# Transposes moved from TensorE to VectorE as 32x32 blocks, and a projection on eight small TensorE tiles

## The chip, the cores and the metric

The kernel runs on one core of one Trainium2 chip. The metric is the device time of one execution in microseconds (us); lower is better. In the profile, PE is TensorE's matmuls, PEld its weight loads, DVE is VectorE, ACT is ScalarE, POOL is GpSimd and SP is SyncE; L472 is line 472 of the kernel that the profile belongs to.

## The reference, cut to what matters

```python
# x: [8, 4224, 192] f32; weight: [8, 7]; w_q, w_k: [192, 64]; w_out: [192, 192]
w   = softmax(weight, axis=-1)                        # 7 taps for each of 8 heads of 24 features
y   = causal convolution of x along the 4224 tokens, with the taps of each feature's head
wq, wk = y @ w_q, y @ w_k
mixed  = (1/sqrt(64)) * (wq @ wk.T) @ y               # no softmax, so the order may be changed
out    = relu(mixed) @ w_out                          # [8, 4224, 192] f32
```

There is no softmax in the mixer. So the kernel forms the small matrix `G = y.T @ y` and from it `M = scale * w_k.T @ G`, and gets `mixed = (y @ w_q) @ M`. Its stages per batch are Y (convolution as a banded matmul), G, M, Q (`y @ w_q`, kept transposed), Z (`relu`), and O (`@ w_out`, then the store).

## The kernel before

The 4224 tokens of a batch are two halves of 2112, worked on side by side. Each half is cut into 18 chunks of 122 tokens. Y leaves tokens on partitions, and Q needs features on partitions, so there is a transpose stage T between them. T runs on TensorE, as matmuls with an identity:

```python
def job_t(b, k):                       # two chunks; 9 such jobs per batch
    def pe(e, bk):
        bank = PS[:, bk, :].bitcast(BF16)
        for q in range(2):
            ...
            for s_ in range(3):        # 3 x 128 of the 384 features (both halves of the tokens)
                last = e.transpose(bank[:, o0 : o0 + m],
                                   Y[0:m, b % 2, c, first : first + 128], IDENT[0:m, 0:m])
        return last
    # evicted: 3 x 244 bf16 columns PSUM -> YT

def job_q(b, k):                       # 488 columns; 5 such jobs per batch
    ...
        for s_, wt in enumerate((WQA, WQB, WQT)):          # full 128x128 weights
            last = e.matmul(PS[:, bk, o0 : o0 + w], wt, y[:, s_], start=..., stop=s_ == 2, ...)
    # evicted: PSUM -> QT
```

A stored tile holds 512 tokens of both halves, four tokens to a partition, and goes out in one DMA:

```python
            elif q == 1:
                src = OUT[:, orr, :, :]                     # 128 partitions x 2 halves x 3072 bytes
                dst = bass.AP(out_t, (b * S + 512 * i) * D,
                              [[4 * D, 128], [HALF * D, 2], [1, 4 * D]])
            ...
            st = P.dma("sp", lambda e: e.dma_start(dst, src), og[orr], evs)
```

All engines run fixed lists of instructions. When the program is built, a scheduler puts one job after another, by a priority for each stage (`KEYS`) and by estimated costs. It gives each eviction from PSUM to the one of VectorE and ScalarE that would finish it first:

```python
COST = {"act": (0.1, 0.833e-3, 0.833e-3), "dve": (0.1, 1.04e-3, 0.52e-3)}   # us, us per element
...
eng = min(("act", "dve"), key=lambda e_: end[e_])
```

## Time and profile before

| | before |
|---|---|
| time, median of the first three runs | 195.45 us (194.65 to 198.22; the run of 198.22 counts as slow) |
| span of the profiled run | 194.0 us, mean granted TensorE clock 0.990 |
| first Y matmul; last eviction; end | 11.76; 188.99; 194.0 us |
| one batch in steady state | 21.8 us |

These are lines from the page of the profile before. The first four are the span in 40 slices, with each digit the busy share of a slice in tenths (PEclk: granted clock). The last two are the chain of work that ended last, by engine and by line, as shares of the span.

```profile
PE   7749999999999999999999999999999999999980
DVE  4864586737856497737966496737856496736740
ACT  2354288876987597876877588876987588875990
PEclk9988999999999999999999999999999999999999
...
PE 89%; DVE 4%; POOL 2%; ACT 1%; issue 1%; POOLq 0%
PE ps L472 13%; PE ps L599 12%; PE ps L442 12%; PE ps L397 11%; PE ps L601 11%; PE ps L493 7%; PE ps L562 6%; PE ps L494 6%; PE ps L495 4%; PE ps L577 4%; DVE shift L296 1%; ACT y L729 1%; POOL xw L205 1%; PE ps L526 1%; DVE xw L369 0%
```

PE is full from slice 4 to slice 38, and the chain stays on it for 89% of the span. The chain in order of time (start, duration, what) shows a repeating mark, a pair of transpose groups:

```profile
55.79 0.65 PE ps L442 x12
...
77.54 0.65 PE ps L442 x12
...
99.28 0.65 PE ps L442 x12
```

So a batch takes 21.8 us. The view by stretches, asked for two of these periods, gives the length and then the busy time of each engine with its number of instructions:

```profile
55.79:77.54 21.75, 21.63 (x227) 16.72 (x225) 14.96 (x29) 16.80 (x34) 4.72 (x6) 1.00 1.37 264
77.54:99.28 21.74, 21.62 (x225) 16.71 (x225) 14.97 (x29) 16.79 (x34) 0.00 (x0) 1.00 1.37 264
```

The columns are PE, PEld, DVE, ACT, POOL, clock, DMA share and GB/s. VectorE and ScalarE have 5 to 7 us to spare in each period. The groups of instructions, with shapes kept apart, show what T and Q cost and what VectorE needs per element (count, then busy us and mean ns of one, then idle time before them and its releasers):

```profile
L734 DVE TENSOR_SCALAR zt<-ps 128x512 bf16<-128x512 f32 x68 | 45.5, 686 | 15.1 <-PE ps L577 5.4 <-PE ps L601 5.1 <-PE ps L562 4.5
L729 DVE COPY yt<-ps 128x732 bf16<-128x732 bf16 x64 | 34.3, 536 | 17.4 <-PE ps L442 9.8 <-PE ps L577 6.8
L442 PE MATMUL ps<-ident,y 122*128 122x122 bf16 x408 | 33.5, 216 | 0.0
L472 PE MATMUL ps<-yt,wall 128*128 128x244 bf16 x192 | 25.6, 268 | 0.3
...
L734 DVE TENSOR_SCALAR zt<-ps 128x64 bf16<-128x64 f32 x9 | 1.9, 222 | 4.1 <-PE ps L562 4.0
```

The mean ns of a matmul is its latency and not its cost, since the next one starts long before it ends. For the cost one reads distances between starts. In the trace they are 54 ns for 122 columns, 83 for 192, 106 for 244, 163 for 384, 183 for 432 and about 216 for 512 (medians). Summed over a batch, everything but T and Q needs about 15.6 us of PE, T needs 2.9 and Q 2.8. That is 21.3 of the 21.8 us.

One more reading matters below. The prediction used the closest starts in the trace, those of the 64-column matmuls in the timeline:

```profile
69.50 0.19 PE L528 MATMUL ps<-gs,wall 128*128 128x64 bf16 x1
69.53 0.19 PE L529 MATMUL ps<-gs,wall 128*128 128x64 bf16 x1
69.56 0.19 PE L530 MATMUL ps<-gs,wall 128*128 128x64 bf16 x1
```

### The profile page before, as it was taken

To read this page: it belongs to the slowest core of one execution; us is meant where nothing else is said; L and a number is where in the kernel's file an instruction comes from. 1 tells how busy PE (TensorE), PEld (TensorE's weight loads), DVE (VectorE), ACT (ScalarE), POOL (GpSimd) and SP (SyncE) were. 2 spreads that over 40 slices of the span, in tenths; PEclk is the share of its full clock that TensorE was granted. 3 is DMA by queue.
4 is the path that set the end of the run, shared out by engine and by line. 5 is a ranking of instruction groups with operands and counts; after the bars stand their busy time and mean duration, and the time that the engine had idled before them with its cause. 6 is when DMAs were issued, how large, how long until landed. Compare 5 with 4: busy or idle time off the path is not lost.

```text
span 194.0 us, 4387 instructions
## 1 busy us (share of the span) xinstructions
PE 181.9 (94%) x1799; PEld 138.3 (71%) x1814; DVE 125.5 (65%) x254; ACT 139.3 (72%) x273; POOL 46.2 (24%) x74
## 2 busy tenths in 40 slices
PE   7749999999999999999999999999999999999980
PEld 2218957788588957788578966788588967789650
DVE  4864586737856497737966496737856496736740
ACT  2354288876987597876877588876987588875990
POOL 6649999992532200000000000000000000000000
PEclk9988999999999999999999999999999999999999
DMA  2996999999999999999999993346044623346098
GB/s 35 182 200 58 192 187 191 272 273 283 269 224 252 276 333 198 271 270 290 263 217 266 286 300 131 124 176 250 0 166 162 268 80 138 114 180 243 0 381 288
DMA packets 47683, 40.21 MB, mean 207 GB/s; under 512 B 37936, under 2 KB 39728, under 8 KB 47664
## 3 DMA queue, kind: packets, MB, share of 16 engines
q0 software_dynamic: 36480, 13.63, 59.1%
q1 hardware_dynamic: 11184, 26.31, 37.3%
q8 instruction: 14, 0.23, 0.4%
q14 instruction: 5, 0.04, 0.1%
HBM read 27.60 MB, written 25.95 MB: 276 GB/s over the span
## 4 chain that ended last, share of the span: by engine, by line
PE 89%; DVE 4%; POOL 2%; ACT 1%; issue 1%; POOLq 0%
PE ps L472 13%; PE ps L599 12%; PE ps L442 12%; PE ps L397 11%; PE ps L601 11%; PE ps L493 7%; PE ps L562 6%; PE ps L494 6%; PE ps L495 4%; PE ps L577 4%; DVE shift L296 1%; ACT y L729 1%; POOL xw L205 1%; PE ps L526 1%; DVE xw L369 0%
## 5 line engine op out<-in xcount | busy, mean ns | idle before, releaser
L729 ACT COPY o_sb<-ps 128x768 f32<-128x768 f32 (+1 forms) x69 | 52.7, 767 | 17.8 <-PE ps L601 15.2
L734 DVE TENSOR_SCALAR zt<-ps 128x512 bf16<-128x512 f32 (+1 forms) x77 | 47.4, 632 | 19.2 <-PE ps L562 8.4
L729 ACT CAST y<-ps 128x432 bf16<-128x432 f32 (+2 forms) x110 | 46.1, 477 | 10.1 <-PE ps L397 9.7
L729 DVE COPY yt<-ps 128x732 bf16<-128x732 bf16 (+1 forms) x65 | 34.6, 534 | 17.4 <-PE ps L442 9.8
L599 PE MATMUL ps<-wall,zt 128*128 128x192 bf16 x272 | 44.9, 247 | 0.0
L601 PE MATMUL ps<-wall,zt 128*128 128x384 bf16 x136 | 44.3, 326 | 0.0
L397 PE MATMUL ps<-xw,band 128*128 128x432 bf16 x128 | 36.7, 351 | 3.3 <-DVE zt L371 3.3
L493 PE MATMUL ps<-y 128*128 128x192 bf16 x144 | 34.8, 249 | 1.1 <-ACT y L729 0.7
L599 PEld LDWEIGHTS ps<-wall,zt 128*128 128x128 bf16 x272 | 27.7, 113 | 10.2 <-ACT o_sb L729 2.0
L494 PE MATMUL ps<-y 128*128 128x192 bf16 x144 | 34.7, 248 | 0.0
L442 PE MATMUL ps<-ident,y 122*128 122x122 bf16 (+1 forms) x432 | 33.7, 216 | 0.0
L205 POOL DMA_DIRECT2D xw<-in_x_dram x32 | 30.2, 1008 | 12.5 <-issue 12.5
L495 PE MATMUL ps<-y 128*128 128x128 bf16 x144 | 31.8, 221 | 0.0
L442 PEld LDWEIGHTS ps<-ident,y 122*128 122x128 bf16 (+1 forms) x432 | 27.5, 97 | 3.5
L472 PE MATMUL ps<-yt,wall 128*128 128x244 bf16 (+1 forms) x216 | 28.5, 265 | 0.3
L729 DVE CAST y<-ps 128x432 bf16<-128x432 f32 x34 | 20.4, 604 | 8.9 <-PE ps L397 8.8
L472 PEld LDWEIGHTS ps<-yt,wall 128*128 128x128 bf16 x216 | 18.2, 97 | 7.5 <-DVE yt L729 4.2
L562 PE MATMUL ps<-qt,m_sb 128*128 128x512 bf16 (+1 forms) x65 | 21.1, 333 | 0.5
L729 ACT CAST qt<-ps 128x488 bf16<-128x488 f32 x25 | 14.1, 565 | 8.7 <-PE ps L472 8.6
L732 ACT ACTIVATE zt<-ps 128x512 bf16<-128x512 f32 (+1 forms) x43 | 19.1, 479 | 1.5 <-PE ps L562 1.5
L493 PEld LDWEIGHTS ps<-y 128*128 128x128 bf16 x144 | 14.2, 99 | 4.8 <-DVE y L729 1.4
L494 PEld LDWEIGHTS ps<-y 128*128 128x128 bf16 x144 | 14.2, 99 | 3.6
(65 smaller groups left out, 150.8 us busy)
## 6 DMA issues: line engine op xcount, KB each, us to landing
out_dram<-o_sb SPq DMA_DIRECT2D x31, 768.0 KB, 6.9
xw<-in_x_dram POOLq DMA_DIRECT2D x24, 384.0 KB, 26.0
xw<-in_x_dram POOLq DMA_DIRECT2D x8, 432.0 KB, 26.2
out_dram<-o_sb SPq DMA_DIRECT2D x8, 96.0 KB, 5.0
out_dram<-o_sb SPq DMA_DIRECT2D x2, 384.0 KB, 4.0
xw<-in_x_dram POOLq DMA_DIRECT2D x8, 45.8 KB, 19.6
xw<-in_x_dram POOLq DMA_DIRECT2D x16, 16.5 KB, 28.8
wst<-in_moe_w_out_dram SPq DMA_DIRECT2D x1, 96.0 KB, 6.1
```

What stands on the lines that cost most here:

```text
L205: return e.dma_start(XW[:, b % NX, slot : slot + n, :], bass.AP(x_t, base, [[D, 128], [CW * D, n], [1, D]]),)
L397: return e.matmul(PS[:, k, 0:432], BAND[:, h, :], rhs, start=True, stop=True)
L442: last = e.transpose(bank[:, o0 : o0 + m], Y[0:m, b % 2, c, first : first + 128], IDENT[0:m, 0:m],)
L472: last = e.matmul(PS[:, bk, o0 : o0 + w], wt, y[:, s_], start=s_ == 0 and j == 0, stop=s_ == 2, skip_group_check=True)
L493: e.matmul(PS[:, 7, 0:192], y[:, 0:128], y[:, 0:192], start=c == 0, **fl)
L494: e.matmul(PS[:, 7, 192:384], y[:, 256:384], y[:, 192:384], start=False, **fl)
L495: return e.matmul(PS[:, 7, 384:512], y[:, 128:256], y[:, 128:256], start=False, **fl)
L562: return e.matmul(PS[:, bk, 0:w], M_SB[:, b % 2, 256 * h : 256 * h + 128], QT[:, b % 2, s0 : s0 + w], start=True, stop=True)
L599: e.matmul(o[:, 192 * h : 192 * h + 192], ZT[:, zr, h, cols], WO1, start=h == 0, stop=False, **kw)
L601: last = e.matmul(o[:, 0:384], ZT[:, zr, 2, cols], WO2, start=False, stop=True, **kw)
L729: last = e.copy(o, i) if eng == "act" else e.tensor_copy(o, i)
L734: last = e.tensor_scalar(o, i, 0.0, None, op0=ALU.max)
```

## The change

The intent is to take the transposes off the engine that bounds the kernel. VectorE can transpose 32x32 blocks inside SBUF. Features then lie on groups of 32 partitions, each group with other tokens. So Q no longer has a contraction over 128 rows. It becomes six accumulating matmuls of 32 rows by 64 columns for each of four row groups (tokens) and two column halves (the two halves of the sequence), which is eight tiles of the array. Chunks shrink from 122 to 120 tokens, so that a chunk is a whole number of four-token groups. The order of the tokens in `QT` changes with that, and so each store now goes out by chunks. Evictions of Y are merged in pairs (864 columns), and a Q job takes four PSUM banks at once.

```diff
-    CW = 122
+    CW = 120
-        rows = 6 + LAST if c0 == NCK - 1 else 128
+        rows = 6 + (LAST if c0 == NCK - 1 else CW)         # loads of 126 partitions
...
+    def job_td(b, k):                                      # three chunks; 6 such jobs per batch
+        def make(bk):
+            return [(
+                YB[:, g, c : c + 3, :].rearrange("p c d -> p (c d)"),
+                Y[:, b % 2, 3 * k : 3 * k + 3, :].rearrange("p c d -> p (c d)"),
+            )]
+        ...  evacs=[(make, ("TD", b, k), 1152, False, "transpose")]      # e.transpose on VectorE
...
+    def job_q(b, g):                                       # 2 such jobs per batch
         def pe(e, bk):
+            for j in range(6):
+                for i in range(4):
+                    r = slice(32 * i, 32 * i + 32)
+                    for h in range(2):
+                        blk = j if h == 0 else (8 + j if j < 4 else 2 + j)
+                        rhs = YB[r, g, :, 32 * blk : 32 * blk + 32]
+                        last = e.matmul(PS[64 * h : 64 * h + 64, bk + i, 0:288], WQ[r, j, :], rhs,
+                                        start=j == 0, stop=j == 5, skip_group_check=True)
...
+            for h in range(2):                             # stores: 14 DMAs per batch, not 5
+                if rem:
+                    parts = [(0, 64, row(h, 17 * CW), [[D, 64], [1, D]])]
+                elif i < 3:
+                    parts = [(0, 128, row(h, 32 * i), [[CW * D, 16]] + chunk)]
+                else:
+                    parts = [
+                        (0, 96, row(h, 96), [[CW * D, 16], [4 * D, 6], [1, 4 * D]]),
+                        (96, 126, row(h, 16 * CW), [[4 * D, 30], [1, 4 * D]]),
+                        (126, 128, row(h, 17 * CW + 64), [[4 * D, 2], [1, 4 * D]]),
+                    ]
```

The priorities of the stages were set anew with it (Y starts earlier, O later: 1.24 instead of 1.05), and the scheduler counts a Q job as 1.6 us.

## The prediction

> **What bounds the kernel now.** TensorE. The chain of waits gives PE 89% of the span. In the stretches by time, every 22 us stretch from 30 to 184 us has PE busy 21.8 to 21.9 us, VectorE about 14.7 and ScalarE 17.3 (together 32.2 of 44). The chain repeats the double transpose group at 55.79, 77.54, 99.28, 121.16, 142.93 and 164.74 us: one batch costs 21.8 us of PE time. Eight of them are 174 us; about 12 us of start and 8 us of drain make up the rest. DMA holds nobody up in steady state.
>
> **Removed from PE, per batch.** By the timeline's starts, a group of six transposes takes 0.32 us, nine groups 2.9 us; Q takes 0.63 us per 488 columns, 2.7 us. Without both, PE needs 16.2 us.
>
> **Added to PE.** Per batch two Q jobs of 48 weight loads and 48 matmuls of 288 columns, eight tiles at once. With perfect overlap a job would be six rounds of about 0.12 us. The densest load-and-matmul pairs in the trace (the 64-column ones of the small product) start 0.03 us apart; 48 pairs at that rate are 1.45 us. The Trainium skill, "TensorEngine Tiling (Array Packing)", Key Properties, says that tiles load weights and multiply in parallel and that a change of tiling mode drains the array; no run here shows either yet. My estimate: 1.65 us a job plus some 0.15 us of drain, 3.6 us per batch. PE then needs about 19.8 us.
>
> **Moved to VectorE and ScalarE, per batch.** The evictions of the transposes go: (34.6 + 3.9)/8 = 4.8 us. Six VectorE transposes of 128x1152 come. The Trainium skill, "Vector Engine (DVE) Microarchitecture Reference", section 3.8, gives one element per cycle and lane. The trace's evictions of 512 and 64 columns (686 and 222 ns) give 1.04 ns per element and 0.16 us fixed, so about 1.35 us each, 8.1 us. Merged Y evictions (864 wide) save six fixed costs, 1.0 us; Q's eviction falls into eleven pieces instead of five and gives that back. Sum 32.2 - 4.8 + 8.1 = 35.5 us, 17.7 us per engine: 90% of a 19.8 us period. That leaves little slack, and Q needs four PSUM banks at once. I add 0.2 us of PE stalls: period about 20.0 us (removed 5.6, added 3.6 and 0.2).
>
> **Lost.** Stores grow from 41 to about 112 issues of about 0.4 us, harmless in steady state, but after the last evictions eight issues instead of two lengthen the tail: about +2 us.
>
> **Sum.** 195.5 - 8 x 1.8 + 2 = about 183 us. Range (8 in 10): 173 to 192 us. Chances: faster by over 2% 0.80, within 2% 0.13, slower 0.07.
>
> **What will show it.** PE still near the limit, period 19 to 20.5 us; a Q job spans 1.4 to 1.9 us from its first to its last start; VectorE transposes 48 x about 1.3 us (some 63 us busy, VectorE total up by some 25 us); last eviction to end about 7 us instead of 5.
>
> **What would make it wrong.** Weight loads of the small tiles in series (over 2.5 us a job) would eat the gain: 193 to 198 us. A Q job under 1 us would hand the bound to VectorE and ScalarE, near 172 us. A VectorE transpose much slower than an element per cycle, or PE waiting for the transposes and four free banks, would move the period to VectorE, above 190 us.

## The result

| | before | after |
|---|---|---|
| time, median | 195.28 us (4 runs, one of them slow) | 186.89 us (4 runs, one of them slow; a fifth is slow too) |
| ratio | | 0.957, 95% interval 0.951 to 0.963 |
| span of the profile; mean clock | 194.0 us; 0.990 | 185.6 us; 0.961 |
| first Y matmul | 11.76 us | 13.70 us |
| last eviction | 188.99 us | 174.70 us |
| last eviction to end | 5.1 us | 10.9 us |
| one batch in steady state | 21.8 us | 19.3 us |

A ratio is the mean time of one kernel's runs over that of the other's runs of the same rounds, so it is not quite the ratio of the medians quoted beside it. Executions over 1.5% slower than the fastest of the same kernel are left out of the means.

The kernel became faster by 4.3%. The table says where: the stretch from the first Y matmul to the last eviction shrank by 16.2 us (177.2 to 161.0), the start grew by 1.9 us and the tail by 5.8 us. The net is 8.4 us.

The same lines of the page, after:

```profile
PE   7907977998998999979989999799899999799500
DVE  4846786998699779985998689968995899767100
ACT  2114739985998789868997899769986998599600
PEclk9995799999999999999999999999999999999965
...
PE 42%; DVE 25%; ACT 18%; DMA 6%; issue 2%; POOL 1%; ACTq 0%
DVE yb L780 19%; PE ps L623 9%; PE ps L403 7%; PE ps L625 7%; PE ps L466 6%; DMA xw<-in_x_dram 6%; ACT o_sb L782 6%; ACT zt L785 5%; ACT y L782 5%; PE ps L586 3%; DVE zt L787 3%; PE ps L517 2%; PE ps L518 2%; PE ps L601 2%; ACT qt L782 2%
```

The chain no longer stays on PE. It goes through three engines, and VectorE's transposes (L780) are the largest single part. The clock falls in slices 4 and 5, after PE stood idle through slice 3, and the last two slices have no compute at all. The fall is deeper than before the change. These are the same 9 us of the start, before and then after (the columns are explained above):

```profile
12.00:21.00 9.00, 8.30 (x76) 6.19 (x75) 5.26 (x10) 5.39 (x13) 8.49 (x16) 0.81 1.06 118
12.00:21.00 9.00, 6.15 (x24) 3.03 (x25) 5.45 (x5) 3.48 (x7) 6.92 (x13) 0.62 0.89 101
```

The mean granted clock was 0.81 and 0.62 there. An estimate from that: 9 us at these clocks are worth 1.7 us less than at full clock before the change, and 3.4 us less after it. The loss varies between profiles. In the traces of the 14 profiles, the first stretch at half clock took 3.4, 6.8 or 10.2 us; it took 10.2 us in the five in which PE stood idle longest before the first Y matmul (5.2 to 5.7 us; 3.3 to 4.6 us in the others). Two profiles, gap_08 and q_one_tile, have a second stretch after 26 us. So single profiles may differ by 1.7 or 3.4 us from this alone. The periods below lie where the clock is 1.00 and are free of it.

Two stretches of two batches each, from one first Q job to that of two batches later:

```profile
82.02:120.61 38.59, 36.70 (x479) 25.41 (x479) 33.04 (x54) 33.39 (x64) 0.00 (x0) 1.00 1.31 268
120.61:159.20 38.59, 36.70 (x480) 25.42 (x479) 33.03 (x54) 33.39 (x64) 0.00 (x0) 1.00 0.58 172
```

A batch takes 19.3 us. PE is busy in 95% of that, VectorE in 86% and ScalarE in 87%. Busy PE counts latencies. By the distances between starts, PE needs 15.6 us for what did not change and, as the next views show, 2 x 0.87 us for Q: 17.35 us. So PE loses some 1.9 us per batch, where before it lost 0.5. The groups of the new work:

```profile
L780 DVE STREAM_TRANSPOSE yb<-y 128x1152 bf16<-128x1152 bf16 x48 | 62.6, 1349 | 0.4
...
L466 PE MATMUL ps<-yb,wq 32*64 32x288 bf16 x768 | 15.1, 285 | 1.2 <-DVE zt L787 0.6 <-DVE yb L780 0.5
```

The timeline of PE around the first Q job (start, duration):

```profile
22.90 0.94 PE L466 MATMUL ps<-yb,wq 32*64 32x288 bf16 x48
23.77 0.26 PE L517 MATMUL ps<-y 128*128 128x192 bf16 x1
```

The next matmul starts 0.87 us after the job's first. In the single records eight matmuls start 3 to 4 ns apart, the next eight follow 123 ns after the first eight (147 ns in most later jobs), and so on for six rounds (0.66 us from the first start to the last). About 0.21 us passes from the last start to the next ordinary matmul, of which 0.12 us are its own 288 columns.

The chain within a period shows the new handover between the engines:

```profile
102.03 0.87 PE ps L466 x48
...
110.18 0.67 DVE zt L787
110.85 3.81 DVE yb L780 x3
114.69 0.32 DVE y L812
115.04 0.69 DVE zt L787
115.76 3.90 DVE yb L780 x3
119.66 0.59 DVE zt L787
120.29 0.39 PE ps L601
120.68 0.87 PE ps L466 x48
```

VectorE transposes for 3.8 to 3.9 us on end, three blocks in a row, and evicts nothing meanwhile. At 119.66 it empties the bank that a Z matmul (L601) waits for, and the next Q job comes after that. The timeline shows PE's wait of 1.04 us:

```profile
120.29 0.39 PE L601 MATMUL ps<-qt,m_sb 128*128 128x512 bf16 x1 [1.04 <-DVE zt L787]
120.61 0.94 PE L466 MATMUL ps<-yb,wq 32*64 32x288 bf16 x48
```

It shows one thing more. The Q job starts 0.32 us after a matmul of 512 columns, where the next ordinary one starts after about 0.216. In all twelve jobs before which PE did not wait, the first start comes 0.09 to 0.12 us later than usual. So a Q job costs PE about 0.1 us on entering as well, and 0.2 of the 1.9 us per batch are not waiting. Last, two stretches of the tail, from the last eviction on:

```profile
174.70:180.20 5.50, 0.00 (x0) 0.00 (x0) 0.00 (x0) 0.01 (x1) 0.00 (x0) 0.79 0.98 333
180.20:185.60 5.40, 0.00 (x0) 0.00 (x0) 0.00 (x0) 0.00 (x0) 0.00 (x0) 0.50 0.48 148
```

For the first half of the tail the DMA engines are full (0.98, 333 GB/s), so they work off a backlog. For the second half they are half idle, while SP issues the last small pieces one after another.

### The profile page after: what moved, and what is told of

The parts are those of the page before. It is cut to its first block, busy times and chain, and to the rows that moved or that the text cites. A ratio compares the mean times of both kernels' runs of the same rounds, so it can differ in the third digit from the quotient of the medians.

```text
span 185.6 us, 4685 instructions
## 1 busy us (share of the span) xinstructions
PE 158.1 (85%) x1934; PEld 105.7 (57%) x1934; DVE 141.1 (76%) x239; ACT 136.5 (74%) x261; POOL 49.2 (27%) x74
## 4 chain that ended last, share of the span: by engine, by line
PE 42%; DVE 25%; ACT 18%; DMA 6%; issue 2%; POOL 1%; ACTq 0%
DVE yb L780 19%; PE ps L623 9%; PE ps L403 7%; PE ps L625 7%; PE ps L466 6%; DMA xw<-in_x_dram 6%; ACT o_sb L782 6%; ACT zt L785 5%; ACT y L782 5%; PE ps L586 3%; DVE zt L787 3%; PE ps L517 2%; PE ps L518 2%; PE ps L601 2%; ACT qt L782 2%
## 5 line engine op out<-in xcount | busy, mean ns | idle before, releaser
L780 DVE STREAM_TRANSPOSE yb<-y 128x1152 bf16<-128x1152 bf16 x48 | 62.6, 1349 | 0.4
L782 ACT CAST y<-ps 128x864 bf16<-128x864 f32 (+3 forms) x80 | 43.1, 631 | 7.3 <-PE ps L403 7.2
L403 PE MATMUL ps<-xw,band 126*128 126x432 bf16 x128 | 33.2, 367 | 4.9 <-DMA xw<-in_x_dram 4.6
L623 PEld LDWEIGHTS ps<-wall,zt 128*128 128x128 bf16 x272 | 26.5, 114 | 15.7 <-ACT y L782 4.4
L787 DVE TENSOR_SCALAR zt<-ps 128x512 bf16<-128x512 f32 (+1 forms) x61 | 30.2, 522 | 4.1 <-PE ps L586 2.0
L785 ACT ACTIVATE zt<-ps 128x512 bf16<-128x512 f32 (+1 forms) x59 | 33.1, 609 | 0.0
L586 PE MATMUL ps<-qt,m_sb 128*128 128x512 bf16 (+1 forms) x80 | 25.6, 343 | 0.4 <-ACT qt L782 0.4
L782 ACT CAST qt<-ps 128x64 bf16<-128x64 f32 (+4 forms) x43 | 14.3, 400 | 11.9 <-PE ps L466 11.6
L782 DVE CAST y<-ps 128x864 bf16<-128x864 f32 x16 | 16.8, 1057 | 4.3 <-PE ps L403 3.6
L601 PE MATMUL ps<-qt,m_sb 128*128 128x512 bf16 (+1 forms) x40 | 13.8, 344 | 3.6 <-DVE zt L787 3.1
L466 PE MATMUL ps<-yb,wq 32*64 32x288 bf16 x768 | 15.1, 285 | 1.2 <-DVE zt L787 0.6
L625 PEld LDWEIGHTS ps<-wall,zt 128*128 128x128 bf16 x136 | 15.3, 112 | 0.0
## 6 DMA issues: line engine op xcount, KB each, us to landing
xw<-in_x_dram POOLq DMA_DIRECT2D x8, 45.0 KB, 16.9
```

What stands on the lines that cost most here:

```text
L403: last = e.matmul(PS[:, k + j, 0:432], BAND[0 : 6 + CW, h, :], rhs, start=True, stop=True)
L586: return e.matmul(PS[:, bk, 0:w], M_SB[:, b % 2, 256 * h : 256 * h + 128], QT[:, b % 2, s0 : s0 + w], start=True, stop=True)
L623: e.matmul(o[:, 192 * h : 192 * h + 192], ZT[:, zr, h, cols], WO1, start=h == 0, stop=False, **kw)
L625: last = e.matmul(o[:, 0:384], ZT[:, zr, 2, cols], WO2, start=False, stop=True, **kw)
L780: last = e.transpose(o, i)
L782: last = e.copy(o, i) if eng == "act" else e.tensor_copy(o, i)
```

## The experiments

All kernels derive from the changed kernel unless said otherwise. Times are medians; the ratio is to the kernel before. The changed kernel has 0.957 (0.951 to 0.963). One of the six runs of retuned was slow.

| run | time, us | ratio (95%) | result |
|---|---|---|---|
| loads_128 | 185.64 | 0.953 (0.949 to 0.957) | correct |
| stores_plain | 181.81 | 0.931 (0.929 to 0.933) | wrong |
| half_transposes | 182.84 | 0.938 (0.933 to 0.944) | wrong |
| q_twice | 199.91 | 1.025 (1.022 to 1.029) | correct |
| stores_two_queues | 187.31 | 0.962 (0.956 to 0.968) | correct |
| gap_08 | 183.59 | 0.942 (0.940 to 0.944) | correct |
| q_cost | 184.17 | 0.947 (0.942 to 0.952) | correct |
| q_four_tiles | 189.24 | one look, state unknown | correct |
| merge_odd | 185.80 | 0.953 (0.950 to 0.956) | correct |
| q_one_tile | 215.67 | one look, state unknown | correct |
| retuned | 178.91 | 0.915 (0.911 to 0.918) | correct |
| retuned_half | 176.97 | 0.906 (0.899 to 0.912) | wrong |

### What sets the period: half_transposes and q_twice

```diff
+            n = 1152 if b == 0 else 576
-                YB[:, g, c : c + 3, :].rearrange("p c d -> p (c d)"),
+                YB[:, g, c : c + 3, :].rearrange("p c d -> p (c d)")[:, 0:n],
```

> Wrong result on purpose: from batch 1 on each VectorE transpose covers 576 of its 1152 columns; order and everything else are the same. It takes 0.6 us from each transpose, 3.6 us of VectorE per batch. Theory P1, the 19.3 us period is set by VectorE and ScalarE and by the blocks of three transposes in which VectorE empties no PSUM bank, while TensorE idles about 1.9 us per batch: the period falls by 1 to 1.9 us, the time to 173 to 179 us. Rival P2, TensorE still sets the period: the period falls by less than 0.4 us, the time stays above 184 us.

```diff
-            for j in range(6):
+            for j, i, h in [(j, i, h) for _ in range(2) for j in range(6) ...]:
```

> The changed kernel with every Q job's 48 matmuls done twice (the second pass starts its sums anew, so the result is right): about 0.9 us of TensorE more per job, 14 us over all. Theory P1: a good part of it falls into time that TensorE idled, up to 1.9 us per batch: 187 to 195 us. Rival P2: it is added in full, about 200 to 202 us. It also measures what a job costs: 96 matmuls should span 1.75 us from the first to the last start if a job costs what it did in the profile.

The groups of half_transposes show that the cut did what it should:

```profile
L781 DVE STREAM_TRANSPOSE yb<-y 128x576 bf16<-128x576 bf16 x42 | 29.6, 750 | 0.2
...
L781 DVE STREAM_TRANSPOSE yb<-y 128x1152 bf16<-128x1152 bf16 x6 | 7.8, 1349 | 0.1
```

It took 3.6 us per batch from VectorE, and the period fell by 0.6 us only (58.60 to 133.30 us is four batches, 18.7 each). The time fell by about 4 us. That is less than P1 expected and more than P2 allowed.

q_twice made a job's first-to-last start 1.40 us instead of 0.66, so it added 1.5 us of PE per batch. The period grew by 2.0 us on average over four batches (61.70 to 146.71 us, 21.25 each). But four of the jobs in that stretch took 1.8 to 3.1 us from first to last start, because PE stopped in the middle of them, 3.4 us in all. The longest stop:

```profile
90.03 0.32 PE L464 MATMUL ps<-yb,wq 32*64 32x288 bf16 x5 [1.42 <-issue]
```

"issue" means that the trace names nothing that PE waited for; the cause was not followed up. The changed kernel has no such stop. In the two batches of q_twice without one (125.57 to 166.29 us) the period is 20.4 us, 1.1 us more than in the changed kernel. So PE's idle time absorbed about 0.4 of the 1.5 us. The time of 199.91 us is near what P2 expected, but it holds the stops.

So both theories fall in their simple form. About a sixth of the time taken from VectorE comes back, and about three quarters of the time given to PE is paid, although neither engine is full. Q is a place where the others wait: in the changed kernel ScalarE and VectorE wait 11.6 and 7.5 us in all for Q's matmuls, and 24.0 and 19.3 us in q_twice, its stops included. What is left as a suspect is the fixed order, in which each engine's place in its list decides what waits.

### The order: gap_08 and q_cost

```diff
         elif kind == "TD":
             t = max([t] + [done[a_].end for a_ in job.after if a_[1] >= 0])
+            k = 6 * job.name[1] + job.name[2] - 1
+            if k % 3 != 2 and k >= 0:
+                t = max(t, done[("TD", k // 6, k % 6)].end + 0.8)
```

> The changed kernel, but the scheduler may place the second and third transpose of a group only 0.8 us after the end of the one before, so that VectorE empties PSUM banks between them instead of transposing for 3.9 us on end; the work is the same. Theory P3, the blocks of three transposes hold up the banks that VectorE would have emptied and TensorE waits for those: the period falls by 0.4 to 1.2 us, the time to 178 to 184 us. Rival P4, the delay comes from the chain transposes, then Q, then its eviction, then Z, whose length the spreading only adds to: the time stays or gets worse, 186 to 191 us.

```diff
-            ("Q", b, g), b + KEYS["Q"][0] + KEYS["Q"][1] * g / 2, 4, pe, 1.6,
+            ("Q", b, g), b + KEYS["Q"][0] + KEYS["Q"][1] * g / 2, 4, pe, 0.9,
```

> The changed kernel with the one cost that the scheduler had badly wrong, a Q job of 1.6 us, set to the 0.9 us of the profile; so the fixed order of all engines is worked out anew from nearly true costs. Theory P5, the 1.9 us that TensorE idles per batch come from an order made for a slower Q: the period falls by 0.4 us or more, the time below 184 us. Rival: the order hardly matters at this load, 185.5 to 188.5 us.

Both edits leave the work as it is and change the lists: their order, and, since the scheduler deals out the evictions as it goes, also which engine does some of them. In gap_08 41 instructions of VectorE evict Y instead of 16, in q_cost seven evictions more go to ScalarE. The busy time of each of the two engines stays within 4 us of the changed kernel's over the whole run.

gap_08 took the ratio from 0.957 to 0.942, and its period was 18.9 us on average over four batches (60.52 to 135.97 us). q_cost came to 0.947, with an interval that just meets that of the changed kernel, and to 18.9 us (57.54 to 133.26). P3 holds on time and period. P5 holds on the period only just (19.3 to 18.9), and the time missed its "below 184" by 0.2 us. What became shorter are PE's waits. The view of waits, for two batches of the changed kernel (82.02 to 120.61 us) and then for the four of gap_08 (us in total, times, longest):

```profile
PE ps L601 <- DVE zt L787: 2.1, 2, 1.0
PE ps L623 <- ACT y L782: 0.5, 1, 0.5
...
PE ps L623 <- DVE qt L785: 1.3, 2, 0.6
PE ps L623 <- ACT o_sb L785: 0.6, 3, 0.2
```

That is 1.3 us per batch before, and with a third entry of 0.2 us 0.5 us per batch in gap_08; q_cost comes to 0.5 too. The wait of the Z matmul for VectorE is gone in gap_08. The rivals (no change, or worse) are out: the lists cost. Which part of them is not shown. gap_08 broke up the blocks of three transposes, but q_cost left them whole (3.9 us each in its trace) and its period is as short.

### Why Q is so cheap: q_four_tiles and q_one_tile

```diff
-            for j in range(6): for i in range(4): for h in range(2):       # eight tiles in turn
+            for h in range(2): for j in range(6): for i in range(4):       # q_four_tiles
+            for i in range(4): for h in range(2): for j in range(6):       # q_one_tile
```

> The changed kernel with the matmuls of a Q job in another order: all of one column half first, so that only the four row tiles can run at once. If the cheap Q job (0.87 us) comes from eight tiles running at once, four at a time cost 12 rounds of about 0.12 us: about 1.5 us from the job's first matmul to the next job's first, 0.6 us more. If the job is bound by the issue of its 48 pairs, the order changes nothing: 0.85 to 0.95 us.

> The changed kernel with the 48 matmuls of a Q job ordered so that the six of one tile follow each other. The profile of the changed kernel shows rounds of eight matmuls that start 3 to 4 ns apart, and 123 ns between two rounds. If matmuls start strictly in program order, six of one tile in a row cost 6 x 123 ns and the job eight times that, 5.9 us, and the whole run gets over 60 us longer. If a tile's matmul may start ahead of an earlier one that waits for another tile, as the 1.14 us of the order of four tiles suggests (1.48 us were expected there), the job stays under 3 us.

A job in q_four_tiles took 1.14 to 1.17 us on the chain in steady state, between the two expectations. In q_one_tile it took 2.77 to 2.84 us on the chain (the second of the run took 3.96 us):

```profile
23.73 2.79 PE ps L464 x48
...
45.83 2.84 PE ps L464 x48
```

The order matters, so the issue of 48 pairs is not the bound; at eight tiles the pairs start 14 ns apart on average. It matters less than strict program order with 123 ns per matmul on a tile would give (1.48 and 5.9 us). The starts of q_four_tiles form two trains of four matmuls, each with 123 ns from four to four, and the second train begins before the first ends. The natural reading is that matmuls of the second column half start ahead of earlier ones that wait for their tile. The records do not name the tile, so this is an inference. With the eight tiles in turn, the job is six rounds of 123 ns and what entering and leaving it cost.

### The tail: stores_plain, stores_two_queues and merge_odd

```diff
-            for h in range(2): ... 14 pieces per batch ...
+            (the stores of the kernel before: one DMA for both halves, consecutive rows)
```

> Wrong result on purpose: the changed kernel, but each stored tile goes out as before the change, one DMA for both halves to consecutive rows (rows land in the wrong place; bytes and row size of 3072 are the same), 41 issues instead of 112. Theory T1, the tail is long because the store pieces are issued one after another on SP[...]: from the last eviction to the end 5 to 6.5 us instead of 10.9, time about 181 to 183 us. Rival T2, the tail is long because batch 7 and the late part of batch 6 leave more bytes to write at the end than the DMA engines can take: the tail stays over 9 us, the time within 1.5 us of 186.9.

```diff
+                    if h == 1 and b >= B - 2:
+                        st = Op("pool", f, evs, dma=(og2[orr], og2[orr].total))   # own semaphores
+                        late.append(st)                                           # after all loads
```

> The changed kernel, right result; for the last two batches the stores of the second half of the tokens are issued by GpSimd, which is idle by then, instead of SP; pieces and bytes are the same. Theory T1a, SP's serial issue (0.5 to 1.9 us a piece, 28 pieces in the last 24 us) makes the tail: from the last eviction to the end falls from 10.9 us to 6.5 to 8 us, the time to about 183 to 184 us. Rival T1b, the pieces themselves[...] make it: the tail stays over 9.5 us and the time within 1 us of 186.9.

```diff
+                    if p1 - p0 < 96:               # pieces of 30, 2 and 64 partitions: both halves at once
+                        if h == 1:
+                            continue
+                        dims = [dims[0], both, dims[-1]]
...                                            # and src takes both halves
```

> The changed kernel, right result; the small store pieces (30 and 2 partitions, and the 64 single rows) go out for both halves of the tokens in one DMA: 11 issues per batch instead of 14, three fewer after the last eviction. Theory T1b, the small pieces make the tail: 1.5 to 3 us less from the last eviction to the end, time 184 to 185.5 us. Rival T3, the tail is long because the last batches' stores as a whole come late and in a crowd, whatever their pieces: the time within 1 us of 186.9.

With the plain stores the tail is 5.5 us, as before the change, with the same compute (last eviction 174.53 us). The stretch from there to the end moves rows of the same size:

```profile
174.50:180.00 5.50, 0.00 (x0) 0.00 (x0) 0.01 (x1) 0.03 (x1) 0.00 (x0) 0.86 0.85 306
```

So the tail is the price of the store pieces, as T1 expected, some 5 us of the whole time, and not of the bytes (T2). In stores_two_queues half of the pieces of the last two batches went out from GpSimd. SP's last issue ended about 4 us earlier in the profile (179.3 instead of 183.3 us), and the tail stayed at 10.8 us. So SP's serial issue alone is not the cause (T1a falls). Merging the small pieces took the tail to 9.0 us, about a third of the excess, which is in line with T1b. The time (185.80 us) missed T1b's range by 0.3 us, and the interval of its ratio, 0.953, overlaps that of the changed kernel. The lists count here too: gap_08 has all the pieces, and its tail was 9.2 us. The small pieces can be costly for their size. On SP's queue the piece of 30 partitions took 1.7 and 1.9 us to issue in two of its four cases in the last 20 us, and 0.59 in the other two, where a piece of 128 took 0.6 to 1.2 us. The Trainium skill, "DMA: Bandwidth & Descriptors", in its section on why a DMA increments its semaphore by 16, says that a DMA of this kind uses the largest number of engines up to 16 that divides the slowest dimension of both its sides, which makes 15 for 30 partitions and 2 for 2. No run here shows the engines one by one. What the rest of the excess is made of stays open.

### The start: loads_128

```diff
-        rows = 6 + (LAST if c0 == NCK - 1 else CW)
+        rows = 6 + LAST if c0 == NCK - 1 else 128
```

> The changed kernel, but the chunk loads fill 128 partitions again instead of 126 (the last two rows are not used). Theory S1, the start is late because a load of 126 partitions is cut into pieces[...]: the first Y matmul starts at about 11.8 us as before the change, not 13.7; the 4-byte packets of the load queue fall from 5744 to about 1000; the whole gets 2 to 3 us faster, about 184 to 185 us. Rival S2, the start is late because of the other new loads (four of the Q weights with 256-byte rows) or by chance: first Y matmul still after 13 us, the time within 1 us of 186.9.

The 4-byte packets of the load queue fell from 5744 to 976. The first Y matmul started at 12.39 us. In the ten profiles with loads of 126 partitions (this change and its variants) it started between 12.83 and 13.70 us, 13.3 on average; in the three with 128 it was 12.39, 12.16 and 12.27. So the loads of 126 partitions cost about 1.0 us at the start, and S1 is right in kind: the width of the loads matters. How the transfers of such a load are shared out was not looked at. Half a microsecond to the 11.76 us before the change remains, and it was not traced. The time missed S1's 184 to 185 us, and the effect on it (0.953 against 0.957) is within the intervals.

### A better version: retuned and retuned_half

retuned puts the findings together: the scheduler's Q cost at 0.88 us, a transpose placed only after the one before it has ended (the gap_08 edit with 0.0 for 0.8), loads of 128, merged small pieces, and new priorities, chosen with a model of the fixed lists in which these costs were put.

```diff
-    "Y": (-0.27, 0.38), "T": (0.24, 1.17), "Q": (0.01, 0.95), "G": (0.03, 0.98),
-    "Z": (0.61, 1.2), "O": (1.24, 0.87),
+    "Y": (-0.22, 0.37), "T": (0.24, 1.17), "Q": (-0.16, 0.71), "G": (-0.05, 0.79),
+    "Z": (0.66, 1.08), "O": (1.07, 0.76),
```

> An attempt at a better version, right result: 128-partition loads, merged small stores, the scheduler's cost of a Q job near the truth (0.88 us), transposes placed one at a time and not in threes, and the priorities of the stages set anew for these costs, with the output stage earlier (1.07 instead of 1.24). If the 1.9 us per batch that TensorE idles and the late crowd of stores come from the fixed order, as gap_08 and q_cost suggest: period 18.0 to 18.7 us, last eviction by 169 us, tail 7 to 9 us, time 175 to 180 us. If the order is near its best and the hand-offs bound it: 182 us or more.

It took 178.91 us, ratio 0.915, and so beats both kernels. The chain and two periods of it:

```profile
PE 78%; DVE 6%; DMA 5%; ACT 4%; issue 1%; POOL 1%; DVEq 0%
```

```profile
55.98:74.26 18.28, 18.23 (x240) 12.64 (x240) 16.20 (x30) 16.91 (x31) 4.75 (x6) 1.00 1.33 278
74.26:92.54 18.28, 18.23 (x240) 12.65 (x240) 16.20 (x30) 16.91 (x31) 0.00 (x0) 1.00 1.33 278
```

The work per batch of VectorE and ScalarE is the same as in the changed kernel within 0.4 us (16.2 and 16.9 us against 16.5 and 16.7). The period is 1.0 us shorter and the chain is PE's again. Over three batches (55.98 to 110.82 us) the view of waits lists none of PE (it lists those over 0.15 us). The last eviction is at 167.54 us and the tail is 8.4 us.

> Wrong result on purpose: the retuned kernel with each VectorE transpose from batch 1 on cut to 576 columns, as half_transposes did to the changed kernel, where it gave about 4 us. Theory P6, it was the order of the work, not the transposes' own time, that kept TensorE waiting, and in the retuned order TensorE has little left to wait for: the gain shrinks to 2 us or less (177 us or more). Rival P7, VectorE's load is the bound in any order: the gain stays 4 us or more (below 175 us).

Cutting the transposes in the retuned order gave 176.97 us, at the edge of what P6 allowed. The period fell by 0.2 us (18.28 to 18.09), against 0.6 us in the changed order. The intervals of the two ratios just overlap, so the size of the gain in time (about 2 us) is not sharp; the periods are. P7 is out: VectorE's load is not the bound in either of the two orders tried.

## Why the prediction was right, and where it was not

The time fell into the range (186.9 of 173 to 192 us) and the direction was right. Its terms, one by one:

1. **What bounds the kernel: right.** T and Q were 5.7 us per batch of a full PE (5.6 in the prediction), and with T gone and Q cheaper the period fell by 2.5 us.
2. **The VectorE transpose: right.** Predicted "about 1.35 us each", measured 1349 ns. The slope from 576 to 1152 columns is (1349 - 750) / 576 = 1.04 ns per element. That agrees with one element per cycle and lane in section 3.8 of the page cited, at the rate that the evictions show.
3. **The Q job: mis-sized by a factor of two.** The step "48 pairs at that rate are 1.45 us. [...] My estimate: 1.65 us a job plus some 0.15 us of drain" measured 0.87 us with the drain. The 0.03 us between pairs was read as a limit of issue. It was only the time that a 64-column matmul needs to stream its columns: the distances grow with the columns (29 ns for 64, 54 for 122, 106 for 244), and the new job has starts 3 to 4 ns apart. The form set aside, six rounds of about 0.12 us, was the true one, plus 0.09 us. Tiles do load and multiply in parallel, as the skill's page says, and the change of mode costs about 0.09 us on leaving the job and about 0.1 us on entering it.
4. **Stalls: mis-sized the other way.** "I add 0.2 us of PE stalls" measured 1.9 us (0.5 before; 0.2 of the 1.9 are the entering of Q). Terms 3 and 4 nearly cancel: about 15.6 + 1.74 + 1.9 = 19.3 us, predicted 20.0. That the period came so close is luck: Q was put 1.9 us too dear and the stalls 1.7 us too cheap. The kernel did not become PE-bound at a lower level; it became bound in part by the fixed lists in which three engines hand work to each other. gap_08, q_cost and retuned show that the lists make a good part of the stalls, since they do the same work in shorter periods (18.9, 18.9 and 18.3 us) with shorter waits of PE. The prediction's own side case, that a Q job under 1 us "would hand the bound to VectorE and ScalarE, near 172 us", failed too: the job was that short and the time was 186.9 us.
5. **The load of VectorE and ScalarE: 33.2 us per batch against the 35.5 predicted.** VectorE's total rose by 15.6 us, not 25, because the scheduler moved other evictions to ScalarE (those of Z on VectorE fell from 47.4 to 30.2 us, and on ScalarE rose from 19.1 to 33.1).
6. **The tail: mis-sized.** "About +2 us" counted issues at the cost of large pieces. It was +5.8 us. stores_plain shows that the store pieces make it.
7. **The start: not in the prediction.** The first Y matmul came 1.9 us later in the profile, about 1 us of it from loads of 126 partitions.

The sum of the prediction was 8 x 1.8 - 2 = 12.4 us. In its place stand 16.2 us between the first Y matmul and the last eviction, less 1.9 us of start, less 5.8 us of tail. Of the 20.0 us that eight shorter periods give (8 x 2.5), 3.8 us are missing between the first Y matmul and the last eviction. By the estimate above, up to 1.7 us of them are the longer stretch at half clock; the rest lies in filling and draining the pipeline and was not taken apart.

## What to carry to other kernels

When the bound engine is relieved by a quarter, the next bound can be the order of hand-offs and not another engine: here three engines at 86 to 95% still lost 10% of a period, and a list made from one wrong cost was worth correcting. Before a test run is read as "the added work is paid in full", look whether the added work ran as planned: in q_twice four jobs stopped midway. A cost estimate for a new instruction shape should first ask what the old shape was limited by; the closest spacing seen is not an issue limit if the instruction's own streaming explains it. Changes of layout are paid at the edges, so cost the first load and the last stores by their pieces and partitions, and not by their bytes.

## What the Trainium skill lacked or had wrong

- "TensorEngine Tiling (Array Packing)" gives the drain at a change of mode no number. Here 0.21 us passed from the last start of a small tile to the next full matmul, 0.09 us more than its 288 columns take, and the first small matmul started 0.09 to 0.12 us later than usual after a full one.
- The same page gives no rate for eight tiles of 32x64 that each load new weights before every matmul. Here they ran six rounds of eight at 123 ns a round, with starts 3 to 4 ns apart, so the loads were hidden entirely. "TensorE: Matmul & The Clock Gate", Part 3, has the 4 ns between starts, and the traces agree.
- The same Part 3 says that matmuls start in strict program order. Jobs ordered by tile took 2.77 us instead of 48 x 123 ns = 5.9 us, and in another order two trains of matmuls ran interleaved. Either matmuls of free tiles overtake, or a tile accepts them faster than its columns stream; the records do not tell which.
- "DMA: Bandwidth & Descriptors" has no cost for a load of 126 partitions instead of 128. Loads of 126 partitions made 5744 packets of 4 bytes where loads of 128 made 976, and the first data was used about 1.0 us later.
- No page gives the price of small store pieces behind a backlog. A piece of 30 partitions (90 KB) held SP's queue for 1.7 and 1.9 us in two of four cases and 0.59 us in the others, and all the pieces cost about 5 us at the end of the run.
